# Linear attention into an ELU MLP: tokens on 64 partitions by nine in a row instead of 128 by four and a rest

## The chip, the cores and the metric

The program runs on one core of a Trainium2 chip. Its time is the device time of one execution in microseconds (us); a run's figure is a median of executions. One execution is also recorded by the hardware profiler, and every duration below is from that record. All matmuls run at the full granted TensorE clock (1.00 in every stretch that is shown).

## The reference

Shapes: B=8 batches, H=8 heads, S=576 tokens, D=64; x has B*S=4608 rows of H*D=512 columns; w_in is 512x2048, w_out is 2048x512; all in float32.

```python
q_s = softmax(q, axis=-1)              # over d, for each token
k_s = softmax(k, axis=2)               # over the tokens
kv  = einsum('bhsd,bhse->bhde', k_s, v)
att = einsum('bhsd,bhde->bhse', q_s, kv)
x   = att.transpose(0, 2, 1, 3).reshape(B*S, 512)
h   = x @ w_in
g   = where(h > 0, h, exp(min(h, 0)) - 1)
out = g @ w_out
```

## The kernel before

**The MLP sets the pace.** The 4608 tokens are cut into nine groups of 512: group j (0 to 7) holds 512 of batch j's 576 tokens, and group 8 holds the 64 tokens that are left of each batch (the "rests"). A group has 16 steps. Step s of group j is `hidden` (four matmuls of 128x512 into one PSUM bank, L778), an exp on ACT (L766, tile ES), a minus one on POOL (L767), a max and min on DVE that gives GT (`elu`, L789), and, three steps later (LAG), `project` (four matmuls of 128x512 into four banks, L799). `hidden` has three banks in turn, so a bank must be released by `elu` before the third `hidden` after it. Four banks hold the projection, and the last one, AB (bank 7), serves everything else. After a group's last `project` its four banks are copied to OSB0 to OSB3 (`evict`, ACT and DVE in turn) and stored by four DMAs on SP's queue (`store`, L817).

**The attention of batch j+1 is worked out beside group j.** q goes through max, subtract, exp, sum and multiply (`qmax`, `qsub`, `qexp`, `qsum`, `qmul`), is turned by a DMA transpose on SP's queue (`turn`, QW<-QS and for the rest QWR<-QSR), and widened to QT (`wide`, on ACT or POOL). k's maximum over the tokens is taken with DVE's transposing reduce (`peak`, `join`), goes out to DRAM and comes back spread over all partitions (`kout` and `kin`, tiles KU, kmax_scratch, NB, on ACT's queue); then `ksub` and `kexp`. `kv` is the sum over tokens of exp(k) times v in bank AB, `kfac` divides it into MB, and `flat:0` to `flat:4` multiply MB with QT in five slices through bank AB, each copied to XT (`xflat`). XT is what `hidden` of the next group reads. `rest` and `xrest` do the same for the 64 tokens that go to group 8. For batch 1 the maximum goes over TensorE (`kturn`, `kacross`, `diag`, `kspread`, `copy`), and four `att` matmuls stand in place of the flats.

**The order is written out by hand.** START is a list of words for everything ahead of the first full step. Then each group has a table of steps, FIRST for group 0, SECOND for group 1, LATER for the others (CHANGED replaces two of its entries in group 2). An entry holds three strings: the words that go between `hidden` and `project`, those between `project` and `elu`, and those after `elu`. A word is a function with its part and, for some, its engine (`qmul:A:dve`; A and B are halves of the heads, R the rest; without an engine it is POOL for `qsub`, `ksub` and `qmul`, ACT for exps and most copies). Each engine and each DMA queue takes its instructions in this order, so a word that waits holds what stands behind it on its engine. Loads, transposes and stores all go through SP's queue; the weights (`w1`, `w2`) go through POOL's queue.

**Layout.** A load brings a half (A, B) or the whole (M) of a tensor as [128 partitions x 4 tokens] in 1024-byte runs, and the 64 tokens that don't fit as two rest pieces (R) of [64 partitions x 4 heads] in 256-byte runs:

```python
dst = t[:, 4 * h0:4 * h1, :].rearrange("p (h r) d -> p h (r d)", r=R)            # R = 4
frm = src[b, h0:h1, 0:SM, :].rearrange("h (p r) d -> p h (r d)", r=R)
...
rows = self.out[j * S:j * S + SM, :].rearrange("(p r) c -> r p c", r=R)[t]        # store: 128 rows
```

Of the kernel before, what the change touches and what calls it, by code (L numbers as in the profile page):

```python
# [27 lines left out]
AB = 7  # L28
# [6 lines left out]
AT = {"rawA": 0, "rawA2": 1, "rawB": 3, "rawB2": 2, "rawS": 7, "rawT": 4,  # L35
      "kturnA": 5, "kturnB": 3, "kvA": 5, "kvB": 6, "pturnA": 6, "pturnB": 4,
      "att0": 5, "att1": 7, "att2": 3, "att3": 6}
START = ("load:K:0:A load:Q:0:A load:K:0:R kmax:A qmax:A load:K:0:B kmax:S kraw:A load:Q:0:B kraw:S "
         "kmax:B kmax:T qsub:A:gp qmax:3 warm:4:3 kturn:A load:K:1:R kacross:A load:V:0:A w1:2:4 "
         "w1:0:2 qexp:A kturn:B load:V:0:R diag:act:A w2:0:2 kmin:S kacross:B kexp:S kraw:T w1:4:6 "  # L40
# [6 lines left out]
FIRST = {  # L47
    0: ("", "", ""),
    1: ("", "", ""),
    2: ("qmax:A", "w2:6:8", ""),  # L50
    3: ("qsub:0 w1:12:14", "qsub:1:dve", ""),
    4: ("", "qmax0:R qexp:A w2:8:12", "qsum:A load:Q:1:B qsub0:R"),
    5: ("", "kturn kacross", "qexp0:R qmul:A qsum0:R"),
    6: ("diag", "qmax:C", ""),
    7: ("qsub:D:dve", "kspread qsub:2 w1:14:16", "hold copy load:V:1:RAB"),
    8: ("qexp:C", "qmulr0:gp ksub:1:dve", "ksub:0:dve load:K:2:MR"),
    9: ("pturn:A", "ksub:3 ksub:R", "qsum:C pwide:A:act"),
    10: ("qmul:B:dve pturn0:R kexp:A", "pwide0:R:act", ""),
    11: ("vconv:A:dve", "rest0 w2:12:13 vconv:R", "ksub:2:dve rcopy0:act"),
    12: ("load:Q:2:ABR pturn:B kexp:R vconv:B:gp", "", "load:V:2:MR pwide:B:act"),  # L60
    13: ("kv:A", "kexp:B kfac:A:dve att:0", "xc:0 w2:13:15 w2:15:16 peak2:A"),
    14: ("kv:B kfac:B:dve", "att:1 qmulr:dve peak2:B", "xc:1"),
    15: ("peak2:R join2 att:3 xc:3", "", "turn:R att:2 xc:2 kout2"),
}
SECOND = {
    0: ("qmax:A", "qsub:0:dve qmax:C", "load:Q:2:MR qsub:1"),
    1: ("qexp:A", "qsub:D", ""),
    2: ("qsub:2", "", ""),
    3: ("kin qsum:A", "qmul:0", "qexp:C wide0:R:act"),
    4: ("", "qsum:C", "qmul:1:dve ksub:2:dve"),  # L70
    5: ("", "load:K:2:MR", ""),
    6: ("qmulr:dve ksub:R:dve", "kexp:R qmul:B:dve", "ksub:3:dve"),
    7: ("rest0 turn:A", "rcopy0:dve", "vconv:B"),
    8: ("", "vconv:R ksub:A", "kexp:B peak2:B"),
    9: ("peak2:R kexp:A", "vconv:A:dve", "turn:R peak2:A"),
    10: ("", "", "turn:B join2"),
    11: ("", "kv:AB", "wide:A:gp"),
    12: ("kfac:AB:dve", "load:K:3:MR wide:R:act", ""),
    13: ("wide:B:gp", "flat:0", "xflat:0:act"),
    14: ("flat:1", "load:V:2:MR xflat:1:dve flat:2", "xflat:2:act"),  # L80
    15: ("kout2 flat:3", "xflat:3:dve", "flat:4 xflat:4:act xrest:act qmax2:A"),
}
LATER = {
    0: ("qsub:0", "", ""),
    1: ("", "kin qsub:1:dve", "vconv:R"),
    2: ("qsub:2", "", ""),
    3: ("qexp:A", "ksub:R:dve ksub:0:dve", "qsum:A"),
    4: ("", "", "qsub:D ksub:1:dve"),
    5: ("", "ksub:3:dve ksub:2:dve", "qexp:C"),
    6: ("", "kexp:A qmul:A:dve", "qsum:C"),  # L90
    7: ("kexp:B", "vconv:A:gp", ""),
    8: ("vconv:B turn:A kexp:R", "qmulr:gp", ""),
    9: ("", "peak2:A kv:AB qmul:B kfac:AB:dve", "wide:A:act peak2:R"),
    10: ("", "", "load:K:3:MR"),
    11: ("flat:0 xflat:0:act turn:R", "wide:R:act", "qmax2:A"),
    12: ("peak2:B join2", "turn:B", "flat:1 xflat:1:act wide:B:gp"),
    13: ("load:Q:3:MR", "flat:2", "qmax2:C xflat:2:act"),
    14: ("", "flat:3", "load:V:2:MR kout2 xflat:3:act"),
    15: ("flat:4", "", "xflat:4:act xrest:dve"),
}  # L100
# [16 lines left out]
class Gen:  # L117
# [57 lines left out]
    def alloc(self):  # L175
# [27 lines left out]
        self.KA = a("KA", [128, H, 64], F32)  # L203
        self.KT2 = [a(f"KT2{i}", [128, 4, 64], F32) for i in range(2)]
# [7 lines left out]
        self.NBR = a("NBR", [128, 4, 64], F32)  # L212
# [8 lines left out]
    def init(self):  # L221
# [14 lines left out]
        op("gp", lambda: g.memset(self.VB[:, :, :, 64:VW], 1.0), (), ["VBA", "VBB"])  # L236
# [5 lines left out]
        op("dve", lambda: v.memset(self.EKR0[0][64:128, :, :], 0.0), (), ["EKR0S"])  # L242
        op("dve", lambda: v.memset(self.EKR0[1][0:64, :, :], 0.0), (), ["EKR0T"])
# [21 lines left out]
    def load(self, which, b, parts, en="sp"):  # L265
# [3 lines left out]
        t, e = bufs[s], self.E[en]  # L269
        for part in parts:  # L270
# [20 lines left out]
    def kmax(self, b, part, en="dve"):  # L291
        v, s = self.E[en], b % 2
        KR = self.KR[s]
        if part in "AB":
            h0 = 0 if part == "A" else 4
            kv = KR[:, 4 * h0:4 * h0 + 16, :].rearrange("p (h r) d -> p h r d", r=R)
            out = self.KA[:, h0:h0 + 4, :]
            KT, kt = self.KT2[h0 // 4], f"KT2{part}"
            self.op(en, lambda: v.tensor_tensor(out, kv[:, :, 0, :], kv[:, :, 1, :], ALU.max),  # L299
                    self.kkeys(b, part), [f"KA{part}"])  # L300
            self.op(en, lambda: v.tensor_tensor(KT[:, :, :], kv[:, :, 2, :],
                                                kv[:, :, 3, :], ALU.max),
                    self.kkeys(b, part), [kt])
# [11 lines left out]
    def span(self, part):
        return {"A": (0, 2), "B": (2, 4)}.get(part, (0, 4))

    def halves(self, name, part):
        return [f"{name}{x}" for x in ("AB" if part == "" else part)]

    def kturn(self, part="", bank=AB):
        pe = self.E["pe"]
        ka = self.KA[:, :, :].rearrange("p h d -> p (h d)")
        f0, f1 = self.span(part)

        def turn():
            for f in range(f0, f1):
                last = pe.transpose(self.bank[bank][:, f * 128:(f + 1) * 128],
                                    ka[:, f * 128:(f + 1) * 128], self.ID32[:, :])
            return last  # L330
        self.op("pe", turn, self.halves("KA", part) + ["ID32"], [f"bank{bank}"])

    def kacross(self, part="", bank=AB):

        v = self.E["dve"]
        f0, f1 = self.span(part)
        self.op("dve", lambda: v.tensor_reduce(
            self.NM[:, f0:f1], self.bank[bank][:, 128 * f0:128 * f1].rearrange(
                "p (f t) -> p f t", f=f1 - f0),
            AX.X, ALU.max, negate=True), [f"bank{bank}"], self.halves("NM", part))  # L340

    def kdiag(self, en="dve", part=""):
        v, a = self.E["dve"], self.E["act"]
        f0, f1 = self.span(part)

# [689 lines left out]
```

## Time and profile before

| | |
|---|---|
| runs | 312.14, 312.81, 313.04 us; median 312.81 us |
| profiled execution | 312.28 us, span of the trace 310.5 us, clock 1.00 |
| first full step starts (`hidden` of group 0) | 20.93 us |
| groups 1 to 8 start | 54.80, 87.84, 120.63, 152.47, 183.74, 215.04, 246.33, 275.37 us |
| span ends | 310.5 us |
| one 128x512 matmul in a steady step | 0.23 us from start to start; a step of eight 1.81 us |

The page gives busy time by engine, the chain of work that ended last, groups of instructions by line and tile, and DMA issues with the time to landing. Names are the program's tiles with the buffer number left out. In the table of windows each line is a stretch of time: its length, busy time and instructions of each engine, the clock, the share of the 16 DMA engines in use and the rate moved. [...]

### The profile page before, as it was taken

The page shows a single profiled execution, that of the slowest core. Times are in us where ns is not written, and L with a number is a line of the kernel's source. Part 1 is how long each engine was busy: PE and PEld are TensorE (multiplying, and loading weights), DVE is VectorE, ACT ScalarE, POOL GpSimd, SP SyncE. Part 2 cuts the span into 40 slices and gives each one's busy share as a digit, 9 for nine tenths or more (in the row PEclk, how much of TensorE's full clock was granted, in tenths as well). Part 3 has the DMA queues.
Part 4 walks back from the last instruction along what each step waited for, and adds up shares of the span by engine and source line. Part 5 has one row for each costly group of instructions (what it writes and reads, how often), then busy time and mean ns, then how long its engine had stood idle before and what let it go on. Part 6 is the DMA issues. An engine that isn't in the chain of part 4 may idle for free.

```text
span 310.5 us, 4547 instructions
## 1 busy us (share of the span) xinstructions
PE 296.0 (95%) x1601; PEld 236.0 (76%) x1601; DVE 243.8 (79%) x420; ACT 177.9 (57%) x295; POOL 174.0 (56%) x229
## 2 busy tenths in 40 slices
PE   3688999999999999999999999999999999999995
PEld 1356876688778868887887888888888888888884
DVE  6999998999879997999799979997895354335541
ACT  1475786558357845694478556955695543334432
POOL 2987985655636843675467636763676333333330
PEclk9999999999999999999999999999999999999999
DMA  7999999998918695439742974152412030003003
GB/s 234 320 352 328 373 338 312 294 320 146 290 41 246 165 255 167 170 60 268 208 170 48 266 223 169 34 129 70 169 34 44 0 137 0 0 2 136 0 1 135
DMA packets 65607, 51.63 MB, mean 166 GB/s; under 512 B 29360, under 2 KB 58288, under 8 KB 65584
## 3 DMA queue, kind: packets, MB, share of 16 engines
q1 hardware_dynamic: 57984, 41.23, 49.4%
q0 software_dynamic: 6400, 8.39, 10.0%
q10 hardware_dynamic: 1200, 1.72, 1.8%
q8 instruction: 12, 0.20, 0.3%
q14 instruction: 11, 0.09, 0.1%
HBM read 38.27 MB, written 9.45 MB: 154 GB/s over the span
## 4 chain that ended last, share of the span: by engine, by line
PE 80%; DMA 8%; DVE 6%; ACT 2%; POOL 1%; SPq 1%; issue 1%; DVEq 0%
PE bank L778 38%; PE bank L799 38%; DMA QWR<-QSR 4%; DMA W2S<-in_moe_w_out_dram 3%; PE bank L709 2%; DMA KR<-in_k_dram 2%; DVE QZ L604 1%; ACT ES L766 1%; PE bank L535 1%; POOL ES L767 1%; DVE GT L789 1%; DVE QS L618 1%; SPq L276 1%; PE bank L652 1%; DVE KA L299 0%
## 5 line engine op out<-in xcount | busy, mean ns | idle before, releaser
L767 POOL TENSOR_SCALAR ES<-ES 128x512 f32<-128x512 f32 x144 | 95.7, 666 | 119.2 <-ACT ES L766 118.8
L799 PE MATMUL bank<-W2S,GT 128*128 128x512 f32 x576 | 154.5, 392 | 1.2 <-DVE GT L789 0.9
L778 PE MATMUL bank<-XT,W1S 128*128 128x512 f32 x512 | 139.2, 394 | 0.2 <-ACT XT L696 0.2
L789 DVE SCALAR_TENSOR_TENSOR GT<-bank,ES 128x512 fp32r<-128x512 f32 x144 | 96.8, 679 | 50.9 <-PE bank L778 42.0
L766 ACT ACTIVATE ES<-bank 128x512 f32<-128x512 f32 x144 | 85.6, 597 | 87.2 <-PE bank L778 86.4
L799 PEld LDWEIGHTS bank<-W2S,GT 128*128 128x128 f32 x576 | 107.2, 188 | 24.0 <-DVE GT L789 1.4
L778 PEld LDWEIGHTS bank<-XT,W1S 128*128 128x128 f32 x512 | 94.1, 188 | 19.7 <-ACT XT L696 0.9
L594 POOL TENSOR_TENSOR QR<-QR,QM 128x512 f32<-128x512 f32 (+3 forms) x24 | 28.7, 1199 | 5.4 <-DVE QM L586 5.2
L600 ACT ACTIVATE QR<-QR 128x1024 f32<-128x1024 f32 (+3 forms) x18 | 19.0, 1060 | 11.6 <-POOL QR L594 10.2
L586 DVE TENSOR_REDUCE QM<-QR 128x16 f32<-128x1024 f32 (+3 forms) x18 | 21.7, 1208 | 0.5 <-DMA QR<-in_q_dram 0.5
L604 DVE TENSOR_REDUCE QZ<-QR 128x16 f32<-128x1024 f32 (+3 forms) x18 | 21.7, 1206 | 0.0
L731 ACT ACTIVATE XT<-bank 128x512 fp32r<-128x512 f32 (+2 forms) x28 | 15.4, 552 | 10.1 <-PE bank L709 9.9
L414 DVE TENSOR_TENSOR KR<-KR,NB 128x512 f32<-128x512 f32 x25 | 17.8, 745 | 0.3
L778 PE MATMUL bank<-XTR,W1S 128*128 128x512 f32 x64 | 16.6, 389 | 0.0
L452 ACT ACTIVATE EK<-KR 128x1024 bf16<-128x1024 f32 x14 | 14.7, 1050 | 0.8 <-POOL KR L414 0.8
L618 POOL TENSOR_TENSOR QS<-QR,QI 128x1024 f16<-128x1024 f32 (+1 forms) x9 | 14.5, 1617 | 1.1 <-DVE QI L606 1.1
L367 DVE TRANSPOSE_TENSOR_REDUCE KM<-KR 128x32 f32<-128x1024 f32 x12 | 14.8, 1237 | 0.4 <-DMA KR<-in_k_dram 0.4
L778 PEld LDWEIGHTS bank<-XTR,W1S 128*128 128x128 f32 x64 | 12.0, 188 | 2.5
L709 PE MATMUL bank<-QT,MB 128*128 128x320 f32 (+5 forms) x48 | 11.8, 306 | 0.8 <-ACT QT L731 0.7
L709 PEld LDWEIGHTS bank<-QT,MB 128*128 128x128 f32 x48 | 8.5, 188 | 5.0 <-ACT QT L731 1.7
L618 DVE TENSOR_TENSOR QS<-QR,QI 128x1024 f16<-128x1024 f32 (+1 forms) x9 | 10.5, 1170 | 0.1
L809 DVE COPY OSB<-bank 128x512 f32<-128x512 f32 x16 | 10.3, 686 | 0.4 <-PE bank L799 0.3
(96 smaller groups left out, 204.9 us busy)
## 6 DMA issues: line engine op xcount, KB each, us to landing
out_dram<-OSB SPq DMA_DIRECT2D x35, 256.0 KB, 2.8
KR<-in_k_dram SPq DMA_DIRECT2D x7, 1024.0 KB, 6.0
VR<-in_v_dram SPq DMA_DIRECT2D x6, 1024.0 KB, 7.4
QR<-in_q_dram SPq DMA_DIRECT2D x5, 1024.0 KB, 7.2
W1S<-in_moe_w_in_dram POOLq DMA_DIRECT2D x8, 512.0 KB, 11.3
QR<-in_q_dram SPq DMA_DIRECT2D x6, 512.0 KB, 8.2
VR<-in_v_dram SPq DMA_DIRECT2D x4, 512.0 KB, 7.7
W2S<-in_moe_w_out_dram POOLq DMA_DIRECT2D x3, 512.0 KB, 10.4
```

Of the source, the lines that this page charges most:

```text
L414: self.op(en, lambda: e.tensor_tensor(kv, kv, m, ALU.subtract), keys + ["NB"], keys)
L586: self.op("dve", lambda: v.tensor_reduce(self.QM[:, g], QR[:, g, :], AX.X, ALU.max), self.qkeys(b, part), self.qstat("QM", part))
L594: self.op(en, lambda: e.tensor_tensor(QR[:, g, :], QR[:, g, :], m, ALU.subtract), keys + self.qstat("QM", part), keys)
L600: self.op("act", lambda: a.activation(QR[:, g, :], QR[:, g, :], AF.Exp), keys, keys)
L604: self.op("dve", lambda: v.tensor_reduce(self.QZ[:, g], QR[:, g, :], AX.X, ALU.add), self.qkeys(b, part), self.qstat("QZ", part))
L618: self.op(en, lambda: e.tensor_tensor(out, src, z, ALU.mult), keys + self.qstat("QI", part), [f"QS{x}" for x in cells])
L709: last = pe.matmul(self.bank[bank][:, a - c0:b - c0], self.MB[f][:, :, :].rearrange("p u d -> p (u d)"), self.QT[:, f, a - f * S:b - f * S ...
L766: self.op("act", lambda: a.activation(ES[:, :], ps, AF.Exp), [f"bank{bank}"], [ek])
L767: self.op("gp", lambda: g.tensor_scalar(ES[:, :], ES[:, :], -1.0, 1.0, ALU.add, ALU.mult), [ek], [ek])
L778: return pe.matmul(ps, self.W1S[:, kc, c * 128:(c + 1) * 128], x[:, kc, 0:SM], start=(kc == 0), stop=(kc == 3))
L789: self.op("dve", lambda: v.scalar_tensor_tensor(self.GT[n % NG][:, :], ps, 0.0, ES[:, :], ALU.max, ALU.min), [f"bank{bank}", ek], [f"GT{n ...
L799: return pe.matmul(self.bank[OB[t]][:, :], self.GT[n % NG][:, t * 128:(t + 1) * 128], self.W2S[:, c, :], start=(c == 0), stop=(c == NCH - 1))
```

## The change

q of every batch, and k and v of batch 0, are loaded as [64 partitions x 9 tokens in a row]: heads 4P and 4P+1 on partitions 0 to 63 and heads 4P+2 and 4P+3 on partitions 64 to 127, in four loads of 295 KB with runs of 2304 bytes, and no rest pieces. k and v of the later batches keep the old layout. Consequences in the code:

- Group j's 512 tokens are now those with r = 0 to 7 of `(p r)`, r = 8 goes to group 8, so the stores address their rows as `[2, 64, 512]` instead of `[128, 512]`. The number of stores and their bytes stay.
- The DMA transposes of q become two of 128x1152 for a batch, in place of two of 128x1024 and one of the rest; QWR, its `wide` and the separate rest multiply go. Batch 1's q is turned on TensorE (`pturn`) with its rest; `rest0` remains for batch 0 alone.
- In START: k's maximum is one strided reduce for a half; `kraw`, `kmin`, `kexp` follow the new layout; `kv_first` takes exp(k) times v in 36 tiles of 64x64 for a half, into two banks; `warm` and `await` are not used.
- Batch 1's k maximum takes the way of the later batches (`peak`, `join`, `kout`, `kin`); its attention is the five flats in steps 14 and 15 of FIRST.
- All tables are new. In LATER, POOL has both halves of `qmul`, two of the `ksub`, both `wide` and `xrest`; ACT has `vconv`. The weights come in other portions.

```diff
+QP = 64
+QN = S // QP
+QF = SM // QP
 ...
+        if which == "Q" or b == 0:
+            for x in "".join({"A": "01", "B": "23", "M": "0123"}.get(x, x) for x in parts):
+                P, a = int(x) // 2, int(x) % 2
+                dst = t[64 * a:64 * a + 64, 2 * QN * P:2 * QN * (P + 1), :].rearrange("p (u r) d -> p u (r d)", u=2)
+                frm = src[b, 4 * P + 2 * a:4 * P + 2 * a + 2, :, :].rearrange("u (p r) d -> p u (r d)", r=QN)
+                ...
+                self.op(en, lambda: e.dma_start(dst, frm), (), cells, dma=f"d_{cells[0]}")
+            return
 ...
+    def kmax(self, part):
+        v, P = self.E["dve"], "AB".index(part)
+        src = self.KR[0][:, 2 * P * QN:2 * (P + 1) * QN, :].rearrange("p (u r) d -> p u d r", u=2)
+        self.op("dve", lambda: v.tensor_reduce(self.KA[:, 2 * P:2 * P + 2, :], src, AX.X, ALU.max),
+                self.firstkeys("K", part), [f"KA{part}"])
 ...
+    def kv_first(self, part, banks):
+        ...
+            for r in range(QN):
+                for a in range(2):
+                    sl = slice(64 * a, 64 * a + 64)
+                    for u in range(2):
+                        x = 2 * P + u
+                        last = pe.matmul(self.bank[banks[a]][64 * u:64 * u + 64, 0:VW], self.EF[sl, r, x, :],
+                                         self.VF[sl, r, x, :], start=(r == 0), stop=(r == QF))
 ...
     def qturn(self, part):
+        sp, hh = self.E["sp"], "AB".index(part)
+        src = self.QS[hh][:, :, :, :].rearrange("p r u d -> p (r u d)")
+        self.op("sp", lambda: sp.dma_start_transpose(self.QW[hh][:, :, :], src),
+                [f"QS{x}" for x in "0123"[2 * hh:2 * hh + 2]], [f"QW{part}"], dma=f"d_QW{part}")
 ...
     def store(self, j):
 ...
-            rows = self.out[j * S:j * S + SM, :].rearrange("(p r) c -> r p c", r=R)[t]
+            rows = self.out[j * S:(j + 1) * S, :].rearrange("(p r) c -> r p c", r=QN)[2 * t:2 * t + 2]
             self.op("sp", lambda: sp.dma_start(rows, self.OSB[t][:, :]),
                     [f"OSB{t}{x}" for x in ("", 0, DM // 2)], [], dma=f"d_OSB{t}")
```

The tables after the change:

```python
FIRST = {
    0: ("peak:R peak:A hold load:Q:1:2", "peak:B qmax:A", ""),
    1: ("", "", "w1:12:14 w1:14:16"),
    2: ("join qsub:0", "qsub:1:dve", "kout"),
    ...
    9: ("ksub:1 qexp:B", "pturn0:R qsum:B ksub:3:dve pwide0:R:act", "load:Q:2:1"),
    10: ("qmul:B", "", "kexp:A ksub:R"),
    11: ("rest0", "rcopy0:act kexp:B vconv:R vconv:A:dve", ""),
    12: ("pturn:B vconv:B:dve pwide:B:act", "", "w2:13:16 kexp:R"),
    13: ("pturn:R load:Q:2:3", "", "pwide:R:act kv:AB"),
    14: ("kfac:AB:dve load:Q:2:0 flat:0", "xflat:0:act peak2:A", "flat:1 xflat:1:act peak2:B"),
    15: ("flat:2 xflat:2:dve load:Q:2:2", "peak2:R hold join2 flat:3 load:V:2:MR",
         "xflat:3:act flat:4 xflat:4:act xrest:dve kout2"),
}
SECOND = {
    ...
    2: ("load:Q:2:0", "", "qsub:0"),
    4: ("", "load:K:2:MR", "ksub:A:dve"),
    5: ("vconv:A", "ksub:R:dve load:Q:2:1 qexp:B", ""),
    8: ("kexp:R vconv:R", "peak2:R load:Q:2:2", ""),
    9: ("kexp:B", "qmax2:A peak2:A qmul:B", ""),
    10: ("", "turn:A", "kv:AB"),
    11: ("turn:B", "kfac:AB:dve", "wide:A:act load:Q:2:3 peak2:B load:K:3:MR"),
    12: ("wide:B:gp join2", "flat:0 xflat:0:act", ""),
    ...
}
LATER = {
    0: ("qsub:0", "", "qsub:2:dve"),
    1: ("", "qsub:3 kin qsub:1", ""),
    3: ("ksub:1:dve", "qexp:A qsum:A", ""),
    4: ("ksub:0:dve qexp:B", "ksub:3", "vconv:B"),
    5: ("", "ksub:R:dve", ""),
    6: ("qsum:B vconv:A", "ksub:2 qmul:A", "turn:A kexp:R kexp:A"),
    7: ("", "kexp:B peak2:B", "qmul:B"),
    8: ("peak2:A", "", ""),
    9: ("qmax2:A", "vconv:R", "turn:B wide:A:gp"),
    10: ("kv:AB kfac:AB:dve", "", "load:Q:3:1"),
    11: ("", "peak2:R", "flat:0 xflat:0:act wide:B:gp"),
    12: ("flat:1", "xflat:1:act", "load:V:2:MR load:Q:3:3"),
    13: ("load:Q:3:0 flat:2 load:Q:3:2", "xflat:2:act", ""),
    14: ("join2 flat:3", "qmax2:B", "xflat:3:act kout2"),
    15: ("flat:4", "xflat:4:dve load:K:3:MR", "xrest:gp"),
}
CHANGED = {
    0: ("", "", "qmax:B qsub:0"),
    2: ("", "", "qsub:2 load:Q:2:0 load:Q:2:1 load:Q:2:2 load:Q:2:3"),
}
```

(In a word such as `peak2` or `load:K:2:MR` the 2 stands for batch j+2.)

More of the change, by code (lines that the diff above doesn't have):

```diff
@@ L47 @@
-FIRST = {
[L48 to L63, printed above, removed]
+AT = {"rawA": 0, "rawA2": 4, "rawB": 6, "rawB2": 7, "rawS": 3, "rawT": 1,
+      "kturnA": 7, "kturnB": 3, "kvA": 1, "kvB": 0, "pturnA": 5, "pturnB": 4,
+      "att0": 5, "att1": 2, "att2": 6, "att3": 3, "kvA2": 2, "kvB2": 6}
@@ L64 @@
 }
 SECOND = {
[L66 to L81, printed above, removed]
+    0: ("qmax:B qsub:3", "", "qmax:A"),
+    1: ("qsub:2:dve", "", "qsub:1"),
+    2: ("load:Q:2:0", "", "qsub:0"),
+    3: ("kin", "vconv:B:dve", "qexp:A qsum:A"),
+    4: ("", "load:K:2:MR", "ksub:A:dve"),
@@ new lines @@
+    5: ("vconv:A", "ksub:R:dve load:Q:2:1 qexp:B", ""),
+    6: ("ksub:2:dve", "", "kexp:A qsum:B"),
+    7: ("", "qmul:1 ksub:3", "qmul:0:dve"),
+    8: ("kexp:R vconv:R", "peak2:R load:Q:2:2", ""),
[3 more added lines that the diff above has]
+    12: ("wide:B:gp join2", "flat:0 xflat:0:act", ""),
+    13: ("flat:1", "", "xflat:1:act load:V:2:MR"),
+    14: ("flat:2 xflat:2:act", "kout2", ""),
@@ L82 @@
+    15: ("flat:3 xflat:3:dve", "", "flat:4 xflat:4:act xrest:dve"),
 }
 LATER = {
[L84 to L99, printed above, removed]
+    0: ("qsub:0", "", "qsub:2:dve"),
+    1: ("", "qsub:3 kin qsub:1", ""),
+    2: ("", "", ""),
+    3: ("ksub:1:dve", "qexp:A qsum:A", ""),
+    4: ("ksub:0:dve qexp:B", "ksub:3", "vconv:B"),
@@ L315, in span @@
[L315 to L331, printed above, removed]
@@ L333, in kacross, with firstkeys @@
[L333 to L352 removed]
+    def firstkeys(self, which, part):
+        later = {"KA": "012", "KB": ("2", "3", "R0", "R1"), "VA": "AB", "VB": ("B", "R0", "R1")}[which + part]
+        return [f"{which}F{x}" for x in {"A": "01", "B": "23"}[part]] + [f"{which}R0{x}" for x in later]
@@ L360, in kpeak @@
+            [f"NM{part}", "ID32"], [f"DG{part}"])
     def kpeak(self, b, part):
@@ L523, in vconv, with kv_mm @@
                         [f"VR0R{i}"], [f"VBR{i}"])
-    def kv_mm(self, part, bank, first=False):
+    def kv_mm(self, part, bank):
         pe = self.E["pe"]
@@ new lines, in qkeys, with qview @@
+    def qkeys(self, name, b, part):
+        ends = ("h0", "h1") if name.startswith("QR") else ("",)
+        return [f"{name}{x}{y}" for x in self.qcells(b, part) for y in ends]
+    def qview(self, t, b, part):
+        v = t.rearrange("p (s r) d -> p s r d", r=QN) if len(t.shape) == 3 else \
+            t.rearrange("p (s r) -> p s r", r=QN)
+        if part == "R":
+            return v[:, :, QF:QN]
+        s0, n = {"A": (0, 2), "B": (2, 2)}.get(part) or (int(part), 1)
+        return v[:, s0:s0 + n, 0:QN if b else QF]
@@ L641, in qturn_first @@
-    def qturn_first(self, part, bank):
+        v, QR = self.E["dve"], self.qview(self.QR[b % 2][:, :, :], b, part)
+        z, i = (self.qview(t[:, :], b, part) for t in (self.QZ, self.QI))
+        self.op("dve", lambda: v.tensor_reduce(z, QR, AX.X, ALU.add),
+                self.qkeys(f"QR{b % 2}", b, part), self.qkeys("QZ", b, part))
+        self.op("dve", lambda: v.reciprocal(i, z),
+                self.qkeys("QZ", b, part), self.qkeys("QI", b, part))
+    def qmul(self, b, part, en="gp"):
+        e, QR = self.E[en], self.qview(self.QR[b % 2][:, :, :], b, part)
+        z = self.qview(self.QI[:, :], b, part).unsqueeze(3).broadcast_to(list(QR.shape))
+        reads = self.qkeys(f"QR{b % 2}", b, part) + self.qkeys("QI", b, part)
+        if part == "R":
+            out, keys = self.QSR[:, :, :].unsqueeze(2), ["QSR"]
+        else:
+            s0, n = {"A": (0, 2), "B": (2, 2)}.get(part) or (int(part), 1)
+            out = self.QS[s0 // 2][:, 0:QN if b else QF, s0 % 2:s0 % 2 + n, :].rearrange("p r u d -> p u r d")
+            keys = [f"QS{s0 + x}" for x in range(n)]
+        self.op(en, lambda: e.tensor_tensor(out, QR, z, ALU.mult), reads, keys)
@@ L646, in qturn_first @@
-        n = src.shape[1]
-        def mm():
-            for j in range(2):
-                for r in range(n):
-                    o = (j * n + r) * 128
-                    last = pe.transpose(ps[:, o:o + 128], src[:, r, 2 * j:2 * j + 2, :]
-                                        .rearrange("p u d -> p (u d)"), self.ID16[:, :])
+        if part == "R":
+            src = [self.QSR[:, 2 * x:2 * x + 2, :] if b == 0 else self.QS[x][:, QF, :, :] for x in range(2)]
+            reads = ["QSR"] if b == 0 else [f"QS{x}" for x in range(4)]
+        else:
+            hh = "AB".index(part)
+            src = [self.QS[hh][:, r, :, :] for r in range(QF)]
+            reads = [f"QS{2 * hh + x}" for x in range(2)]
@@ L654, in mm @@
+        def mm():
+            for i, x in enumerate(src):
+                last = pe.transpose(ps[:, i * 128:(i + 1) * 128], x.rearrange("p u d -> p (u d)"),
+                                    self.ID16[:, :])
             return last
-        self.op("pe", mm, (["QSR"] if part == "R" else [f"QS{x}" for x in {"A": "01", "B": "23"}[part]]) + ["ID16"], [f"bank{bank}"])
+        self.op("pe", mm, reads + ["ID16"], [f"bank{bank}"])
     def qwide_first(self, part, bank, en="act"):
-        a = self.E["act"]
@@ L743, in mm @@
             return last
-        self.op("pe", mm, [f"MB{f}" for f in range(4)] + ["QTR"], [f"bank{bank}"])
+        self.op("pe", mm, [f"MB{f}" for f in range(4)] + ["QTRA", "QTRB"], [f"bank{bank}"])
     def xcopy_rest(self, b, bank, en="act"):
```

357 lines of the change are left out of this document (145 added, 212 removed), and 9 rows, old and new, of the table START.

## The prediction

> **What bounds the kernel now.** I read the page's busy times and chain first, then the windows cut at the starts of the groups.
>
> ```profile
> PE 296.0 (95%) x1601; PEld 236.0 (76%) x1601; DVE 243.8 (79%) x420; ACT 177.9 (57%) x295; POOL 174.0 (56%) x229
> ...
> PE 80%; DMA 8%; DVE 6%; ACT 2%; POOL 1%; SPq 1%; issue 1%; DVEq 0%
> ```
>
> ```profile
> 20.93:54.80 33.87, 32.83 (x195) 24.91 (x191) 32.04 (x56) 23.18 (x41) 25.73 (x33) 1.00 1.28 338
> 54.80:87.84 33.04, 32.49 (x181) 25.83 (x180) 30.35 (x57) 18.76 (x31) 19.22 (x23) 1.00 0.95 245
> 87.84:120.63 32.79, 32.12 (x177) 25.45 (x176) 31.06 (x49) 21.36 (x35) 18.49 (x24) 1.00 0.81 203
> 120.63:152.47 31.84, 31.69 (x177) 25.56 (x176) 28.77 (x48) 20.47 (x34) 18.84 (x24) 1.00 0.67 172
> 152.47:183.74 31.27, 31.27 (x177) 25.72 (x176) 28.31 (x48) 20.62 (x34) 18.87 (x24) 1.00 0.62 173
> ```
>
> Columns are length, then PE, PEld, DVE, ACT, POOL busy, clock, DMA share, GB/s. From group 4 on TensorE has no gap (31.27 of 31.27), so nothing is to be won there, only lost. Groups 0 to 3 hold 33.87, 33.04, 32.79 and 31.84; DVE is 92 to 95% full in the first three. Ahead of them lie 20.93 us of START, which wait on loads. One wait shows in the chain from 96 to 118 us:
>
> ```profile
> 107.04 6.28 DMA QWR<-QSR
> ...
> 113.81 0.51 PE bank L709 x2
> ```
>
> The last thing before group 2's flat is the transpose of the rest, which the change removes.
>
> **The sum, all but the stores** (against 312.28, the profiled execution; it lies 0.5 below the median of 312.81, and I add that back at the end).
>
> START. The eight k and q loads bring the same bytes; only their shape differs. The bounds come from the load rate:
>
> ```profile
> 2.60:5.00 2.40, 0.26 (x1) 0.27 (x2) 1.14 (x9) 0.00 (x0) 0.00 (x0) 1.00 1.06 367
> ...
> 11.20:12.20 1.00, 0.44 (x2) 0.20 (x2) 0.97 (x3) 0.00 (x0) 1.00 (x3) 1.00 1.21 272
> ```
>
> The first is 128-partition loads alone, the second a stretch with 64-partition rest pieces. Thirteen pieces of 295 KB and k's rest, 3.96 MB, precede the end of v's part 0. At 367 GB/s that takes 10.8 us, so it lands near 13, ahead of the 14.3 of v's second half before; at 272 it takes 14.6 and lands near 17, some 2 to 3.5 us later than kv needs it. The 272 belongs to 256-byte runs, the new ones are 2304 bytes, nearer to the 1024-byte row; I take the first: START 0 (0 to +3.5). DVE's strided maximum (1.34 us for 1152 elements, between the rows of 1.21 for 1024 and 1.47 for 1280) replaces four operations of 0.68 to 0.85 for a half, and the 72 small kv matmuls lie behind loads; nothing for either. [...]
>
> Group 0: kturn (0.40), kspread (0.24), one of two kv passes (0.26) go, and waits on late w2 portions around its end (0.27, 0.27, 0.40, 0.48) with the new order of weights: -2.32. Against that, flat:3, its copy, flat:4 and its copy now follow each other on one bank in step 15, two round trips that no other work covers: 1.2 to 2.1, taken 1.65. Net -0.65. Group 1: rest0 goes, -0.40. Group 2: the wait of the fence above, 0.84, and what a DVE 2 us lighter gives back, 0.65: -1.5. Group 3: its own wait of this kind, 0.31, and 0.24: -0.55. From group 3 on POOL carries about 24 us instead of 18.9 (another qmul of 1.9 us, a ksub, a wide of 1.04); where they come together they delay the minus one by 0 to 0.3 a group, +0.55 in all. Sum -2.55: 309.7.
>
> **The stores.** They keep number, bytes and place, and I would cost them at nothing but for their new form.
>
> ```profile
> out_dram<-OSB SPq DMA_DIRECT2D x35, 256.0 KB, 2.8
> ...
> QW<-QS SPq DMA_TRANSPOSE x12, 3.2
> ...
> QWR<-QSR SPq DMA_TRANSPOSE x7, 4.5
> kmax_scratch<-KU ACTq DMA_DIRECT2D x6, 2.0 KB, 4.2
> ```
>
> ```profile
> 159.20:161.40 2.20, 2.20 (x12) 1.81 (x11) 2.14 (x5) 2.05 (x3) 0.97 (x2) 1.00 1.04 374
> ```
>
> This is a stretch with stores alone: all 16 engines busy (1.04) at 374 GB/s, about 23 GB/s for each, 0.7 us for a store. How is a transfer dealt out to 16 engines? ACT's queue has 1200 packets on the page (q10): 6 of 16 rows from KU, 6 of 128 for NB, 128 of the last store make 992. The 208 left are 13 transfers times 16: I read one closing packet from each engine, also where a transfer is only 16 rows of 128 bytes. So they seem to be cut by the outermost count, not by bytes. All of before's transfers have 16, 64 or 128 there; the new store's destination is `[2, 64, 512]`, and an even cut of two gives two engines. The bounds: the nearest row by size, 0.7 us (L824's `64x2x512` lands in 2.4 like the others, but its outermost count is 64); and two engines at 23 GB/s, 262 KB / 46 = 5.7 us, 22.7 for the four. I take the second, since 2 can't be cut in 16 and no row shows another cut. [...]
>
> What is queued behind: a group's stores are issued at +5.9 us (158.3 - 152.47), the first needs 1.45 beside its own transfer (2.16 from issue to landing, less 0.7), so the fourth lands at +30.0. Everything later on SP's queue has a sixteenth of its bytes on each of these two engines, behind them. That a transfer waits for the one ahead shows in the rows: QWR, issued behind a load of k, lands after 4.5, QW after 3.2.
>
> - Groups 3 to 6: `turn:A` (step 6) lands at +30.5 instead of about +18; `wide:A` (POOL, 1.04 x 9/8 = 1.2) ends at +31.7. POOL stands before it with the minus one of the next step behind, and `flat:0` needs it; `flat:0` was due at 12 steps of 1.81 and kv's 1.0, +23.0. TensorE waits 8.7, four times: 34.8.
> - Group 2: the four q loads of step 2 are behind the stores; the two that `qmax2:A` (DVE, step 9) reads land at +31.6, then 1.34, a GT 0.68 and kfac 1.6 stand before `flat:0`: +35.2 against 23.0, 12.2.
> - Group 1: the load of k (step 4, 1.18 MB, 3.2 us) lands at +33.3; `peak2:R` (DVE, step 8) waits for it with the GT of step 8 behind, 0.86 and 0.68, so `hidden` of step 11 starts at +34.8 instead of +20.2: 14.6.
> - Group 0 has no stores before it; groups 7 and 8 have no consumer behind them, and the last stores (+29.5 of group 8) meet two engines nearly empty: 0.
>
> Sum 61.6: 371.3, and with the 0.5 of the median 371.8. An engine at 28 GB/s, a fifth over any row, takes 4.0 off each of six groups (348); the slowest row of stores, 332 / 16 = 20.8, adds 2.6 each (387), and START's bound up to 3.5 more.
>
> **Rivals.**
> - *Stores on 16 engines* (0.17): 309.7 + 0.5 = 310.2, faster. For: every row of before, L824 above all; against: none has an outermost count that 16 doesn't divide. It decides if one store lands in under 4 us.
> - *Stores on 16 engines, and the 64-partition loads at 225 to 272 GB/s* (0.13): START +2.1 to +5.6, 312.3 to 315.8. For: the 272 row; against: its short runs.
> - *Stores on two engines, but transposes not held by them* (0.04): groups 3 to 6 lose nothing, 337. Against: QWR's 4.5.
> - *As forecast* (0.66): own range 348 to 390.
>
> **How the numbers follow.** A measurement of this kernel tells 0.3% (0.9 us) from no change. Faster is the first rival, 0.17; the second lies half within 0.3% (0.06) and half over it (0.07); the others are slower: 0.66 + 0.04 + 0.07 = 0.77. The range must hold 0.8: 0.66 less a tail of 0.03, the third and the second rival, 312 to 390; left out are the first and the tail.
>
> **What would show it.** Right: out_dram<-OSB with a median landing of 13 to 22 us instead of 2.8; windows with a DMA share near 0.13 at 45 GB/s for some 20 us in each group from 1 on; PE idle before L682 (the flats) or L751 (`hidden`) released by QW, QT or GT in groups 1 to 6 of 9 to 15 us, and none in 7. START's first full step near 21 us, group 0 near 33.2 us long. Wrong: stores that land in 3 us, or groups 3 to 6 at 31.3.

## The result, and the profile after

The changed kernel takes 401.05 us (398.83 to 402.68, four runs) against 312.93 for the kernel before in the same job: a ratio of 1.281 (95% interval 1.273 to 1.289). The forecast was 371.8 with a range of 312 to 390. The direction and the mechanism that the forecast put first (stores on two engines) were right; the loss is 88 us where 59 were forecast, and the time lies outside the range, for three reasons that are worked out further down: slower loads, a longer group 0, and TensorE's clock after its waits. The profiled execution is 401.85 us, its span 400.0.

The page of the changed kernel, busy times, chain, and the group of the flats (L681):

```profile
PE 313.9 (78%) x1630; PEld 246.7 (62%) x1630; DVE 233.3 (58%) x399; ACT 168.9 (42%) x277; POOL 193.0 (48%) x239
...
PE 53%; DMA 26%; POOL 7%; DVE 6%; SPq 5%; issue 2%; ACT 1%; DVEq 0%
...
L681 PE MATMUL bank<-QT,MB 128*128 128x320 f32 (+5 forms) x56 | 16.2, 354 | 49.1 <-POOL QT L706 47.9
```

DMA has gone from 8% to 26% of the chain. TensorE idles 49.1 us ahead of the flats alone, 47.9 of them until POOL has widened q (L706). The windows by group, of the changed kernel (columns as in the prediction; groups 0, 1, 3 and 4):

```profile
27.42:68.31 40.89, 34.11 (x190) 25.46 (x190) 34.85 (x57) 20.26 (x34) 24.83 (x29) 0.96 1.21 294
68.31:117.14 48.83, 33.86 (x177) 26.71 (x176) 30.73 (x52) 19.51 (x31) 20.55 (x23) 0.86 0.65 155
...
165.09:207.22 42.13, 33.57 (x177) 26.93 (x176) 25.94 (x46) 19.16 (x31) 22.74 (x27) 0.88 0.67 119
207.22:250.82 43.60, 34.29 (x177) 27.39 (x176) 25.64 (x47) 19.16 (x31) 22.80 (x27) 0.88 0.65 128
```

Two things are new besides the lengths: TensorE's granted clock is below 1.00 (0.86 to 0.96 in these rows), and its busy time in groups 3 and 4 is 1.9 and 3.0 us longer than before for the same 177 matmuls. (The DMA share is above 1.00 in some rows; in the prediction's row of 128-partition loads it is 1.06, with SP's queue alone moving data.) All parts, in us (the forecast by its own steps; "both DMA edits" is e3_both below):

| part | before | forecast | after | both DMA edits |
|---|---|---|---|---|
| START | 20.93 | 20.93 | 27.42 | 21.24 |
| group 0 | 33.87 | 33.22 | 40.89 | 38.99 |
| group 1 | 33.04 | 47.2 | 48.83 | 32.39 |
| group 2 | 32.79 | 43.5 | 47.95 | 33.23 |
| groups 3 to 6 | 31.84, 31.27, 31.30, 31.29 | 40.1 each | 42.13, 43.60, 42.01, 43.06 | 32.66, 32.70, 32.67, 31.56 |
| group 7 | 29.04 | 29.04 | 29.02 | 29.04 |
| group 8 and the end | 35.1 | 35.1 | 35.1 | 35.1 |

Group 3 shows how a wait comes about. The chain of the changed kernel there:

```profile
181.92 0.03 POOL ES L740
181.94 13.53 DMA QW<-QS
195.48 0.05 issue
195.53 1.15 POOL QT L706
196.69 0.14 issue
196.82 0.60 PE bank L681
197.43 1.71 PE bank L751 x4
...
201.10 0.92 PE bank L751 x4
```

The transpose takes 13.53 us from issue to landing (3.2 before) and lands 30.4 us after the group's start; +30.5 was forecast. The same stretch in windows (stores alone, the wait, just after it, later):

```profile
171.50:180.00 8.50, 8.50 (x38) 6.85 (x37) 7.53 (x12) 7.59 (x11) 6.19 (x9) 1.00 0.13 42
188.50:196.50 8.00, 0.00 (x0) 0.00 (x0) 0.58 (x3) 0.00 (x0) 0.97 (x1) 0.63 0.44 105
196.80:200.30 3.50, 3.48 (x10) 2.92 (x11) 2.17 (x4) 1.52 (x3) 2.58 (x4) 0.50 1.03 314
200.30:207.00 6.70, 6.70 (x32) 5.55 (x31) 4.07 (x10) 2.77 (x5) 1.44 (x4) 0.97 1.09 243
```

While only stores run, the DMA share is 0.13, two engines of sixteen, at 42 GB/s. After the wait the granted clock is 0.50 for some 4 us (3.5 to 6.1 us in groups 1 to 6) and then 1.00 again, and `hidden`'s four matmuls take 1.71 us in the chain instead of 0.92.

Group 0 has waits of its own. The chain goes through the exchange that spreads the maximum of batch 1's k over all partitions by way of DRAM (KC is a tile of `join`, L394 is `ksub`):

```profile
34.38 1.09 DVE KC L366
36.22 6.72 DMA kmax_scratch<-KU
42.95 6.38 DMA NB<-kmax_scratch
...
49.96 1.75 DVE KR L394
51.72 0.61 DVE GT L762
52.37 1.21 PE bank L751 x4
```

The exchange takes 13.1 us. On DVE `ksub` stands 2.8 us for NB with a GT behind it, and `hidden` on TensorE waits 2.86 us for that GT.

### The profile page after: what moved, and what is told of

Same layout as the page of the kernel before. It is cut to its first block, busy times and chain, and to the rows that moved or that the text cites. A ratio compares the mean times of both kernels' runs of the same rounds, so it can differ in the third digit from the quotient of the medians.

```text
span 400.0 us, 4563 instructions
## 1 busy us (share of the span) xinstructions
PE 313.9 (78%) x1630; PEld 246.7 (62%) x1630; DVE 233.3 (58%) x399; ACT 168.9 (42%) x277; POOL 193.0 (48%) x239
## 4 chain that ended last, share of the span: by engine, by line
PE 53%; DMA 26%; POOL 7%; DVE 6%; SPq 5%; issue 2%; ACT 1%; DVEq 0%
PE bank L751 25%; PE bank L772 24%; DMA QW<-QS 17%; SPq L277 4%; DMA KR<-in_k_dram 3%; DMA VR<-in_v_dram 3%; PE bank L681 3%; POOL QS L609 2%; DMA kmax_scratch<-KU 2%; DMA NB<-kmax_scratch 2%; DVE GT L762 1%; POOL QT L706 1%; POOL KR L394 1%; SPq L293 1%; POOL ES L740 1%
## 5 line engine op out<-in xcount | busy, mean ns | idle before, releaser
L751 PE MATMUL bank<-XT,W1S 128*128 128x512 f32 x512 | 147.5, 412 | 18.1 <-DVE GT L762 18.0
L751 PEld LDWEIGHTS bank<-XT,W1S 128*128 128x128 f32 x512 | 100.2, 199 | 43.9 <-DVE GT L762 21.7
L681 PE MATMUL bank<-QT,MB 128*128 128x320 f32 (+5 forms) x56 | 16.2, 354 | 49.1 <-POOL QT L706 47.9
L681 PEld LDWEIGHTS bank<-QT,MB 128*128 128x128 f32 x56 | 12.7, 229 | 55.0 <-issue 49.9
L706 POOL CAST QT<-QW 128x1152 fp32r<-128x1152 f16 x11 | 12.6, 1142 | 54.0 <-DMA QW<-QS 54.0
L583 POOL TENSOR_TENSOR QR<-QR,QM 128x576 f32<-128x576 f32 (+3 forms) x25 | 29.2, 1178 | 10.0 <-DVE QM L576 9.8
L609 POOL TENSOR_TENSOR QS<-QR,QI 128x1152 f16<-128x1152 f32 (+1 forms) x14 | 29.5, 2109 | 2.8 <-DVE QI L596 2.8
L576 DVE TENSOR_REDUCE QM<-QR 128x18 f32<-128x1152 f32 (+3 forms) x18 | 21.6, 1198 | 11.7 <-DMA QR<-in_q_dram 11.7
L589 ACT ACTIVATE QR<-QR 128x1152 f32<-128x1152 f32 (+3 forms) x18 | 18.9, 1055 | 10.7 <-POOL QR L583 10.6
L594 DVE TENSOR_REDUCE QZ<-QR 128x18 f32<-128x1152 f32 (+3 forms) x18 | 21.7, 1207 | 0.0
L394 POOL TENSOR_TENSOR KR<-KR,NB 128x512 f32<-128x512 f32 x12 | 16.1, 1338 | 1.5 <-DMA NB<-kmax_scratch 1.5
L394 DVE TENSOR_TENSOR KR<-KR,NB 128x512 f32<-128x512 f32 (+1 forms) x15 | 12.7, 855 | 3.0 <-DMA NB<-kmax_scratch 3.0
```

Of the source, the lines that this page charges most:

```text
L394: self.op(en, lambda: e.tensor_tensor(kv, kv, m, ALU.subtract), keys + ["NB"], keys)
L576: self.op("dve", lambda: v.tensor_reduce(self.qview(self.QM[:, :], b, part), QR, AX.X, ALU.max), self.qkeys(f"QR{b % 2}", b, part), self.q ...
L583: self.op(en, lambda: e.tensor_tensor(QR, QR, m, ALU.subtract), keys + self.qkeys("QM", b, part), keys)
L589: self.op("act", lambda: a.activation(QR, QR, AF.Exp), keys, keys)
L594: self.op("dve", lambda: v.tensor_reduce(z, QR, AX.X, ALU.add), self.qkeys(f"QR{b % 2}", b, part), self.qkeys("QZ", b, part))
L609: self.op(en, lambda: e.tensor_tensor(out, QR, z, ALU.mult), reads, keys)
```

## Experiments

The two DMA faults first, each alone, then together, and the first alone in the kernel before.

**e1_stores_64rows.** Each store is sent as two of one token index each.

```diff
-            rows = ...rearrange("(p r) c -> r p c", r=QN)[2 * t:2 * t + 2]
-            self.op("sp", lambda: sp.dma_start(rows, self.OSB[t][:, :]), ...)
+            for u in range(2):
+                rows = ...rearrange("(p r) c -> r p c", r=QN)[2 * t + u]
+                self.op("sp", lambda: sp.dma_start(rows, self.OSB[t][64 * u:64 * u + 64, :]), ...)
```

> The changed kernel with each store of [2, 64, 512] sent as two DMAs of [64, 512] (64 stores instead of 32, same bytes and rows). Theory A, a store whose outermost count is 2 runs on two DMA engines and holds everything behind it on SP's queue: out_dram<-OSB lands in 2 to 4 us, groups 1 to 6 fall from 48.8, 48.0, 42.1, 43.6, 42.0 and 43.1 us to 31.2 to 33 each, the 27.4 us of START and the 40.9 of group 0 stay: 321 to 326 us. Rival B, it is the 64-partition loads of q that hold the queue in every group: over 380.

Measured 329.57 us (ratio to before 1.052, 1.048 to 1.056). Group 3, in windows:

```profile
134.92:167.60 32.68, 31.80 (x178) 25.46 (x176) 25.88 (x47) 19.17 (x31) 22.78 (x27) 1.00 0.74 178
```

Groups 1 to 6 are 32.78, 33.20, 32.68, 32.76, 32.67 and 31.56. START (28.11) and group 0 (40.83) stay late, as expected; the total is 3.6 us over the expected band: groups 1 to 5 stay at 32.7 to 33.2, and START and group 0 are 0.6 us longer together than in the changed kernel. The stores' form costs 71.5 of the 88 us.

**e2_loads_128part and e3_both.**

```diff
-                dst = t[64 * a:64 * a + 64, 2 * QN * P:2 * QN * (P + 1), :].rearrange("p (u r) d -> p u (r d)", u=2)
-                frm = src[b, 4 * P + 2 * a:4 * P + 2 * a + 2, :, :].rearrange("u (p r) d -> p u (r d)", r=QN)
+                dst = t[:, QN * X:QN * (X + 1), :].rearrange("p r d -> p (r d)")
+                frm = src[b, 2 * X:2 * X + 2, :, :].rearrange("u (p r) d -> (u p) (r d)", r=QN)
```

> The changed kernel with its 295 KB loads (q always, k and v of batch 0) going to 128 partitions with one run of 2304 bytes each, in place of 64 partitions with two runs; bytes, number of DMAs and run length stay. Heads are paired otherwise by this, so the output is not the reference's. Theory A, loads to 64 partitions run at 228 GB/s because of the partitions: rate near 365 again, first full step at 20.5 to 22.5 us instead of 27.4, group 0 several us shorter as the weights and the exchange of k's maximum come earlier; the stores still cost as before: 385 to 394. Rival B, the rate comes from the run length or the number of descriptors, or START is late for its compute: first full step stays at 26 to 28, 399 to 403.

> Both edits together: the stores of 64 rows and the loads to 128 partitions (heads paired otherwise, so not the reference's output). If the two causes are all there is: 309 to 314 us, START near 21, group 0 at 33 to 36, later groups 31.2 to 32. If the new order of words has a cost of its own (POOL fuller, group 0's maximum by the DRAM exchange): 315 to 322, and it shows in which group.

e2 measured 390.35 us (ratio 1.247, 1.242 to 1.252), e3 321.98 (1.028, 1.023 to 1.033). START of the changed kernel and of e2, loads only:

```profile
3.00:17.00 14.00, 7.93 (x15) 3.35 (x16) 8.85 (x12) 2.31 (x4) 5.17 (x5) 0.88 1.05 236
```

```profile
3.00:12.00 9.00, 5.47 (x10) 2.18 (x11) 6.97 (x10) 1.36 (x2) 3.46 (x3) 0.96 1.02 372
```

The engines are as busy (1.05 and 1.02), at 236 against 372 GB/s: a packet of 2304 bytes takes 172 ns against 93 (medians of the same stretches). The first full step starts at 20.90 in e2. In e3, START and groups 1 to 6 are near before, but group 0 is 38.99 and groups 2 to 5 are 0.4 to 1.4 over; so the new order of words has a price of its own, the second of e3's expectations. In e2 group 0 is 40.00 us: against what was expected, the faster loads shorten it by only 0.9.

**e7_before_64part.** The load shape alone, in the kernel before.

```diff
+            if b == 0:
+                def halves():
+                    e.dma_start(dst[0:64], frm[0:64]).then_inc(self.sem(name), 16)
+                    self.count[name] += 16
+                    return e.dma_start(dst[64:128], frm[64:128])
```

> The kernel before with the six loads of batch 0's q, k and v (512 KB, 1024-byte runs) each sent as two DMAs, partitions 0 to 63 and 64 to 127; layout, run length and bytes stay. Theory A, partitions alone set the rate: the loads run near 228 GB/s instead of 349 to 367, first full step at 24 to 26 instead of 20.9, 316 to 319 us. Rival B, long runs or two runs for a partition made the new loads slow: 20.5 to 21.5, 312 to 314.

```profile
3.00:15.00 12.00, 6.85 (x14) 3.70 (x14) 6.82 (x19) 1.59 (x3) 5.30 (x6) 1.00 1.14 235
```

235 GB/s with 1024-byte runs: the rate doesn't come from the run length or the new layout, and with e2, whose loads have the size and number of the changed kernel's, the 64 partitions are left. 321.24 us (1.027, 1.023 to 1.031), over the expected 316 to 319: START came at 23.65, less late than expected, but group 0 grew to 40.55, with a wait of 5.4 us for GT at its start and a clock of 0.92.

**e8_two_queues.** e1 with the upper half of the partitions loaded from ACT's queue.

```diff
+                en2 = "act" if a and b == 0 else en
+                self.op(en2, lambda: self.E[en2].dma_start(dst, frm), (), cells, dma=f"d_{cells[0]}")
```

> e1_stores_64rows (328 us span) with those loads of batch 0 that go to partitions 64 to 127 issued on ACT's queue, the others on SP's, so that both halves of the partitions are written at the same time. Theory G, each half of the partitions has a limit of its own near 228 GB/s: together 300 to 370 GB/s, first full step at 22 to 25 instead of 28.1, 323 to 327. Rival H, the engines take the two queues' packets in turn and gain little: 26.5 to 28.5, 328 to 331.

```profile
3.00:17.00 14.00, 8.72 (x14) 3.65 (x15) 9.63 (x14) 5.24 (x7) 5.77 (x5) 1.00 1.06 262
```

262 GB/s, START at 26.41, 329.49 us beside e1's 329.57: the small gain of rival H (that the engines take the two queues' packets in turn was not shown). Two queues on two halves ran at 262 GB/s where the changed kernel's one queue had 236 in the same stretch, 11% more, not a second half.

**e4_before_2outer and e12_before_4outer.** The kernel before, with nothing changed but the rows that a store addresses.

```diff
-            rows = ...rearrange("(p r) c -> r p c", r=R)[t]
+            rows = ...rearrange("(p r) c -> r p c", r=2 * R)[2 * t:2 * t + 2]        # e4: [2, 64, 512]
+            rows = ...rearrange("(p r) c -> r p c", r=4 * R)[4 * t:4 * t + 4]        # e12: [4, 32, 512]
```

> The kernel before with one edit: each store addresses its rows as [2, 64, 512] instead of [128, 512] (rows of a batch come out in another order; same bytes and number). Theory A: the stores take 22 to 23 us a group on two engines and hold q's transposes: groups 1 to 6 at 41 to 49 us each, START and group 0 as before (20.9, 33.9), clock under 1.0 after the waits: 375 to 398 us. Rival B (the cost needs the new loads or words too): under 330.

> The kernel before with each store addressing its rows as [4, 32, 512] (rows of a batch in another order; same bytes and number). Theory A, as many engines as the outermost count: 92 GB/s while stores run alone, 11.4 us for a group's four, the last landing near +19 of a group, so q's transposes are hardly held: groups 3 to 6 at 31.3 to 33, 313 to 322 us. Rival (any count that 16 doesn't divide falls to two engines or one): as e4_before_2outer, 385 or more.

e4 took 389.72 us (1.243, 1.238 to 1.249), e12 329.88 (1.055, 1.051 to 1.058). Stores alone, e4 and then e12:

```profile
161.00:167.00 6.00, 6.00 (x28) 4.97 (x27) 5.96 (x10) 5.37 (x8) 4.14 (x5) 1.00 0.13 51
```

```profile
242.00:250.00 8.00, 8.00 (x37) 6.64 (x36) 7.93 (x12) 6.75 (x10) 5.80 (x8) 1.00 0.27 102
```

An outermost count of 2 gives a share of 0.13 and 51 GB/s, of 4 gives 0.27 and 102: here the count is the number of engines. The forecast's reading of closing packets holds too: SP's queue has 57984 packets before, 57536 in e4 and 57600 in e12, which is 14 and 12 fewer for each of the 32 stores. e12's four stores take 12.4 to 13.2 us a group where 11.4 were expected, and its groups 1 and 2 are 39.6 and 38.3 (waits of 3.2 us behind the load of k and 4.0 behind q's transpose), so it is 8 us over its band.

**e5_warm_in_wait.** Is the rest of a wait's price the clock? `warm:30` sends 30 matmuls of 128x512 whose result nobody reads.

```diff
-    11: ("", "peak2:R", "flat:0 xflat:0:act wide:B:gp"),
+    11: ("", "peak2:R", "warm:30 flat:0 xflat:0:act wide:B:gp"),          # in groups 3 to 6
```

> The changed kernel with 30 dummy matmuls (128x512 into bank AB, which flat:0 overwrites) ahead of flat:0 in groups 3 to 6, where TensorE waits some 8.5 us for q's transpose behind the stores. Theory C, after an idle wait TensorE runs at half clock for a while, so a wait costs 1.6 to 2.9 us more than its length: clock 1.00 through these groups, and each 1.2 to 2.9 us shorter (42.1, 43.6, 42.0, 43.1 to about 40 to 41.5), 392 to 396 in all. Rival D, the extra time after the wait is the pipeline of ACT, POOL and DVE filling again: unchanged, 399 to 403.

394.98 us against 401.05 (ratios to before 1.262, 1.256 to 1.267, and 1.281). Groups 3 and 4:

```profile
165.18:205.43 40.25, 38.90 (x207) 31.01 (x206) 25.98 (x47) 19.16 (x31) 22.71 (x27) 1.00 0.65 111
205.43:246.75 41.32, 38.98 (x207) 31.02 (x206) 25.66 (x47) 19.15 (x31) 22.78 (x27) 1.00 0.68 134
```

With idle time filled the clock stays at 1.00 in these two groups (0.88 in the changed kernel) and groups 3 to 6 shrink from 170.8 to 163.7 us in all, though they do 30 matmuls more each. Theory C. Group 5 shrank by only 0.2; TensorE still waits 2.05 us at `flat:0` there, 1.4 us later after the group's start than in the changed kernel. In the changed kernel the waits at `flat:0` in groups 3 to 6 are 8.56 to 9.31 us, and the clock after them is 0.50 for 3.5 to 5.9 us.

**e6_words and e9_qmax_later.** What is left in groups 2 to 5 of e3.

```diff
-    7: ("", "kexp:B peak2:B", "qmul:B"),                    # e6, LATER
+    7: ("", "kexp:B peak2:B", "qmul:B:dve"),
-    "... vconv:R vconv:A:dve"  "pturn:B vconv:B:dve ..."    # e6, FIRST
+    "... vconv:R vconv:A"      "pturn:B vconv:B ..."
-    9: ("qmax2:A", "vconv:R", "turn:B wide:A:gp"),          # e9, LATER
-    10: ("kv:AB kfac:AB:dve", "", "load:Q:3:1"),
+    9: ("", "vconv:R", "turn:B wide:A:gp"),
+    10: ("kv:AB kfac:AB:dve", "", "load:Q:3:1 qmax2:A"),
```

> e3_both (stores of 64 rows, loads to 128 partitions, heads paired otherwise, so not the reference's output) with three words moved: in LATER the second half of qmul from POOL to DVE, in FIRST both vconv from DVE to ACT. Theory E, what is left over 313 is the new order of words: in groups 3 to 6 POOL's run of ksub and two qmul makes kfac late (32.7 to 31.4 to 32.0 each), and in group 0 DVE is full, 35.1 of 39.0 us (39.0 to 37 to 38.3): 316.5 to 319.5. Rival F, group 0 waits only for the exchange of k's maximum through DRAM and groups 3 to 6 for something else: group 0 within 0.4, 321 to 323.

> e3_both (heads paired otherwise, so not the reference's output) with one word moved in LATER: qmax2:A, a DVE reduce of 1.34 us that stands ahead of kfac in step 9, goes behind kfac, to the end of step 10. Theory E2, the 0.89 us that TensorE waits at flat:0 in each of groups 2 to 5 is this reduce ahead of kfac: those groups 32.7 to 31.7 to 32.0 each, 317.5 to 319.5. Rival (POOL's run of qmul and ksub alone makes kfac late): wait and groups unchanged, 321 to 323.

e6 failed: 324.71 us against e3's 321.98, intervals of the ratio overlapping, groups 3 to 5 at 33.0 and group 0 at 40.4. POOL got lighter and kfac no earlier: DVE now has the multiply ahead of it. In group 0 the chain goes through ACT, where exps stand behind both conversions; but TensorE's wait behind the exchange is also 0.7 us longer than in e3 (2.42 against 1.74), and that is half of the 1.4 us. e9 was right: 318.58 us, groups 2 to 5 at 32.06, 31.52, 31.53, 31.55. In e3's waits from 125.85 to 158.51 us, TensorE waits for MB; e9's group 3 has no gap left (31.52 of 31.52):

```profile
PE bank L681 <- DVE MB L550: 0.9, 1, 0.9
```

```profile
126.42:157.94 31.52, 31.52 (x177) 25.54 (x176) 25.77 (x47) 19.17 (x31) 22.78 (x27) 1.00 0.65 178
```

So the price of groups 2 to 5 is a DVE reduce that can wait, standing ahead of kfac. e9's group 0 is 40.63 us with the very words that took 38.99 in e3; what differs in the traces is the wait behind the exchange (2.66 against 1.74) and the clock (0.96 against 1.00).

**e10_no_exchange and e11_no_peak.** Group 0 of e3.

```diff
-    "kout" (step 2) and "kin" (step 6) of FIRST; NB is set to zero instead       # e10
-    "peak:R peak:A", "peak:B" (step 0) and "join" (step 2) of FIRST, too         # e11
```

> e3_both (heads paired otherwise, so not the reference's output) without kout and kin in FIRST: batch 1's k has zero subtracted instead of its maximum, and nothing waits for the trip through DRAM; the reduces (peak, join) stay. Theory I, the 12 us of this trip beside the weights hold DVE, and the whole of what follows, in group 0: group 0 at 36 to 37.5 instead of 39.0, 319 to 320.5. Rival (DVE's load alone sets group 0): 38.5 to 39.2, 321.5 to 323.

> e10_no_exchange without batch 1's reduces too (peak and join in FIRST, some 6 us of DVE). Theory: with the trip gone DVE's load at the start of group 0 is the rest of its excess over 33.9: another 1.5 to 3 us, group 0 at 34 to 35.5, 316.5 to 318.5. Rival (the end of group 0, flats and pturn on one bank): within 0.5 of e10_no_exchange.

Group 0 of e3, e10 and e11:

```profile
21.24:60.23 38.99, 32.92 (x190) 24.41 (x190) 35.14 (x57) 20.30 (x34) 24.33 (x28) 1.00 1.10 298
```

```profile
21.42:61.30 39.88, 35.70 (x189) 27.16 (x190) 35.41 (x57) 20.17 (x34) 23.45 (x28) 0.90 1.04 286
```

```profile
21.37:57.83 36.46, 32.67 (x189) 24.42 (x190) 31.93 (x47) 20.22 (x34) 24.48 (x28) 1.00 1.12 310
```

e10 (319.89 us; ratio 1.025, 1.020 to 1.029, against e3's 1.023 to 1.033) doesn't decide: its profiled group 0 ran at a clock of 0.90, which alone adds 2.8 us of busy time to TensorE. e11 (319.02 us; 1.020, 1.017 to 1.023) is at 1.00 and 2.5 us shorter than e3, with DVE 3.2 us lighter, though longer than the 34 to 35.5 expected. So by this pair of executions reduces and exchange together hold 2.5 of the 5.1 us by which e3's group 0 exceeds before's. The traces show the exchange's part: seven profiled executions have FIRST as the changed kernel has it, and in them TensorE's wait for the GT behind NB and the length of group 0 grow together (1.72 and 38.97 us in e8, 1.74 and 38.99 in e3, 2.03 and 40.00 in e2, 2.66 and 40.63 in e9, 2.83 and 40.83 in e1, 2.86 and 40.89 in the changed kernel, 3.27 and 41.30 in e5). Neither e10 nor e11 has this wait (in e10 an earlier one is 2.24 us, where e3 has 1.09). The clock is 1.00 in the first two and 0.96 in the others. What the reduces cost alone, and the 2.6 us that e11 leaves, stay open.

## Why the prediction was right or wrong

**Right: the stores, as a mechanism and as waits.** The forecast took two engines at 46 GB/s and 22.7 us a group; the stores of a group take 21.8 to 22.7. Its waits of TensorE were 14.6, 12.2 and four of 8.7; the trace has 14.58, 12.84, 8.56, 9.31, 8.63 and 8.60, together 62.5 against 61.6, and none in group 7. That groups 1 and 2 came near is in part luck. In group 1 both ends of the wait lie 1.8 us later than priced (+22.0 to +36.6 against +20.2 to +34.8). In group 2 the path that was priced (q, `qmax2:A`, GT, kfac) gave MB at +35.4 against +35.2, but `flat:0` was released by QT, 1.1 us later, since SP could issue q's transpose only at 140.82 (+23.7). One thing behind the waits was not foreseen: SP itself stands still. In the changed kernel's timeline of SP's queue

```profile
170.98 9.61 SPq L790 DMA_DIRECT2D out_dram<-OSB  x4
181.94 12.51 SPq L615 DMA_TRANSPOSE QW<-QS  x2
```

four issues that took 1.82 us now take 9.61. In groups 1 and 2 blocked issues (5.0 us for one load) stand in the chain ahead of the loads of k and q, which still landed near their forecast (+35.2 against +33.3, +32.2 against +31.6). The sign that was named for this, a median landing of 13 to 22 us, could not be read: the record has no landing for the 32 stores on two engines (its median of 2.4 is that of the last three). The DMA share of 0.13 was the sign that served.

**Wrong, step by step** (30.5 us between 371.3 and 401.85 in the profiled execution):

- *START 0 (0 to +3.5): it was +6.5.* The step that failed is the choice between the two rows of rates. The new loads were put beside the 128-partition row because of their long runs; they belonged to the 64-partition row (272), and even below it, at 236. With 128 partitions START is 20.90 (e2). Why 64 partitions are slower, the runs do not show. The second rival had these loads at 225 to 272 GB/s, and was short of their price too (+2.1 to +5.6); no row of before shows its 225, and the loads ran at 236 over START's 3 to 17 us (235 in e7).
- *Group 0, net -0.65: it was +7.0.* The sum counted TensorE's insertions and waits and left out DVE, which the windows showed at 32.04 of 33.87 us, and the exchange, which it put at nothing where it took `kturn` and `kspread` off. The change puts peak and join on DVE and makes 34.9 to 35.1 of it, and the exchange through DRAM holds TensorE for 2.86 us; e11 gives 2.5 us back without both. Some 1.9 us of the 7.7 missed (40.89 against e3's 38.99) go with the longer wait for NB and the clock of 0.96, not with the loads of START: e8 has those too, and 38.97.
- *No term for the clock.* A wait was priced at its length. TensorE comes back at a clock of 0.50 for 3.5 to 6.1 us. Its busy time in groups 1 to 6 is 204.5 us, and 191.1 in e1, for the same work at a clock of 1.00: the clock costs 13.4 us, most of the 16.4 by which these six groups passed their forecast. In groups 3 to 6 the difference is 8.7, of which e5 gave back 7.1.
- *Group 2 -1.5, group 3 -0.55, later +0.14 each: they were +0.4, +0.8, +1.4, +1.4 and +0.3 without the stores (e3).* The gain was real but half the size, and paid back: with the DVE word moved behind kfac (e9, 1.15 us a group) they are -0.7, -0.3, and +0.25 each. POOL was named as the tight engine, and it was the place of that one word. In the changed kernel no wait for MB is left in groups 3 to 6, since QT comes later still, so this fault cost little of the time measured. Group 1's -0.40 held: -0.65.

The range failed for the first three, which all lie on one side: the bounds of the unknown load rate ended at 272, nothing was set aside for what follows a wait, and nothing for the exchange.

## What to carry to other kernels

Read a DMA's access pattern outermost dimension first: here a store with an outermost count of 2 ran on two engines (DMA share 0.13; 42 GB/s in the changed kernel, 51 in e4), and a transpose behind such stores on the queue took 13.53 us to land instead of 3.2, so split it into transfers with a large outermost count (64 gave a share of 0.87, 128 one of 1.04). Load 128 partitions whenever the layout allows it, since loads to 64 ran at 236 GB/s instead of 372 and a second queue brought them to 262 only. When you price a wait of TensorE of several us, add what the lower clock costs after it (13.4 us in groups 1 to 6 here, after waits of 8.6 to 14.6 us), and when you move work into a group, sum every engine of that group, not only the one on the path, and price what replaces each thing that you take away.

## What the runs showed of the hardware

- A store of 128 rows ran on two engines with an outermost count of 2 (51 GB/s), on four with 4 (102) and on all 16 with 128 (374); the DMA shares were 0.13, 0.27 and 1.04.
- Stores from 64 partitions, with an outermost count of 64, ran at 204 GB/s with the DMA share at 0.87 (e1, 142.2 to 147.0 us), from 128 at 374.
- Loads to 64 partitions ran at 235 GB/s with 1024-byte runs (e7) and at 236 with 2304, and with all engines busy (DMA share 1.14 and 1.05); to 128 partitions at 367 with 1024-byte runs and at 372 with 2304 (e2; 1.06 and 1.02).
- The issue of a DMA blocked: with the stores on two engines the third or fourth store of a group held SP for 3.6 to 9.0 us, and the transpose behind them for up to 10.1, where a store's issue took 0.33 to 0.58 before.
- After TensorE idled for 8.6 to 14.6 us the granted clock was 0.50 for the next 3.5 to 6.1 us of dense matmuls. In group 0 a wait of 2.66 us was followed by 0.51 for 3.5 us (e9, 46.5 to 50.0), while 1.00 followed one of 2.42 (e6).
